# 256-byte starts for the tiles that TensorE reads, and a multiplication moved to ScalarE, in a routed expert kernel behind linear attention

## The chip, the cores and the metric

The kernel runs on one core of a Trainium2 chip. The metric is the device time of one execution in microseconds. Before the change the median of three runs is 739.91 us (738.52 to 740.43).

## The reference

Two stages, all in float32. The first is a linear attention over 8 batches, 8 heads, 576 positions and head dimension 64: queries and keys go through a feature map of 256 features (a projection of 128, the largest magnitude subtracted, exponentials of both signs), and a position's output is its features times the sum of key features by values, divided by a normalizer. The second is a mixture of experts on the 4608 tokens of width 512 that come out: a gate picks one of 8 experts for each token, by its own logits or, where a local gate says so, by taking over the choice of the token before, and the token passes through that expert's two layers:

```python
def phi(x):
    proj = np.einsum('bhsd,df->bhsf', x, w_phi)
    proj = proj - np.max(np.abs(proj), axis=-1, keepdims=True)
    return np.concatenate([np.exp(proj), np.exp(-proj)], axis=-1)
...
e = fresh_e if s == 0 or local_gate[b, s] < 0.5 else prev_e
p = softmax(logits[b, s])
h = np.maximum(x[b, s] @ w1[e], 0.0)      # 512 -> 1024
out[b, s] = p[e] * (h @ w2[e])            # 1024 -> 512
```

## The kernel before

**Two stages on the clock.** The front stage (`step`, `proj`, `qtr`, `kv`, `num`, `gate`) walks over 72 pairs of 128-position chunks, writes the tokens to HBM as `xs`, and scatters token numbers and probabilities into one list for each expert, `lst`. The expert stage takes tokens from these lists in slots: a slot is an expert and one to four tiles of 128 tokens. Two *advance slots* of three tiles each (`EARLY`) are planned in the front stage from the lists as far as they are filled; they run while the planning of the rest (`plan_main`, many small VectorE instructions, then gathers by GpSimd) goes on beside them. Then come four slots of four tiles, four of three, one of two, and between them two *paired slots*, in which two experts share one tile.

**What a slot does.** Its expert's weights come as eight pieces of 128x1024 (`load`, L1002 on, through SyncE's queue): four of the first layer, four of the second. `split` (L1023 on) makes two tiles of each piece: ScalarE rounds it to `whi` (L1032), VectorE writes the rest `wlo = wraw - whi` (L1035). Tokens, gathered by GpSimd as `xg`, are transposed by TensorE and split the same way into `xhi` and `xlo` (`parts`, L1150, L1151). For the first advance slot the same split is made in the front stage by `half` (L509, L511).

`three` (L1153 to L1157) is the expert layers' inner product: three matmuls into one PSUM accumulation, high by high, high by low and low by high.

```python
mm(o, ah, bh, start=first, stop=False)   # L1155
mm(o, ah, bl, start=False, stop=False)   # L1156, or as the operands fall
self.last_pe = mm(o, al, bh, ...)        # L1157
```

The first of the two inputs is the stationary operand (128 columns, fetched by a weight load of its own, which the profile calls PEld), the second the moving one. In `layer1` the weights are stationary and the tokens move, as 512, 384 or 256 columns with four, three or two tiles; a weight piece serves two blocks of 128 hidden units, four slices of the input and the three products, 24 matmuls. ScalarE applies the rectifier and writes `hh` (L1200), VectorE writes the rest `hl` (L1201). In `layer2` the hidden values are stationary and the weights move, always 512 columns; for each tile of tokens 24 matmuls (eight blocks, three products) fill one PSUM bank. VectorE then multiplies the bank by the tokens' probabilities into `y` (L1254), and GpSimd scatters `y` to the output by an indirect DMA (L1257). Paired slots use L1168 instead of `three`, whole float32 operands, and take their pieces straight from DMA into `whi` and `wlo`.

**Order.** TensorE's order in the front stage is the program's; from the advance slots on, a list scheduler orders each engine's instructions, led by `issue_after` and by `marks`, the last instruction of a kind on each engine, which `past` puts in front of the next split. `spare` asks for the next weight piece whenever one is used up. In the advance slots the PSUM banks of the second layer come from the pool `psb` (tag `nm`, two banks, shared with small results of the planning); later slots have a pool `psr` of their own.

**Where the tiles lie.** The allocator puts every tile at a multiple of 32 bytes of its partition. Left pools follow on the many small constants, right pools come from the far end. Start addresses, and what is left past a multiple of 256 (all tiles of a kind agree in that, and all steps inside them that a matmul takes are multiples of 256):

| tiles | pool | start addresses | past a multiple of 256 |
|---|---|---|---|
| `whi`, `wlo`, eight each | `moe_early`, left | 22176 to 83616 | 160 |
| `whi`, `wlo`, two each | `moe_wl`, left | 112288 to 124576 | 160 |
| `whi`, `wlo`, three each | `moe_wr`, right | 188384 to 208864 | 224 |
| `xhi`, `xlo` | `moe_x2`, right | 212960, 221152 | 224 |
| `hh`, `hl` | `moe_h2`, right | 149280, 165664 | 32 |
| `kvs`, three (front stage) | `back2`, left | 112288, 114528, 116768 | 160, 96, 32 |

Weight pieces take the pools' places in turn (`wpool`), so most slots have some pieces left and some right. Of the 864 matmuls of 512 columns in the second layer, 642 read left weights and 222 right ones; in the first layer 312 of 384 matmuls with 512 columns, 432 of 576 with 384 and 48 of 96 with 256 load left weights. Those that the prediction shows: the first four-tile slot's first layer (from 357.11 us) has two left pieces and then two right ones; the two-tile slot's (from 708.36) the same; the three-tile slot's first layer from 402.50 has left pieces only, the three-tile slot's second layer from 612.87 as well, and the stretch from 658.74 in a four-tile slot's second layer is three right pieces.

Of the kernel before, what the change touches and what calls it, by code (L numbers as in the profile page):

```python
# [7 lines left out]
F32 = mybir.dt.float32  # L8
F32R = mybir.dt.float32r
BF16 = mybir.dt.bfloat16  # L10
I32 = mybir.dt.int32
AF = mybir.ActivationFunctionType
# [22 lines left out]
FILL = 6  # L35
KVLAG = 1
QUOTA = 16

STEP = "step"

# [29 lines left out]
class Kernel:  # L70
# [427 lines left out]
    def halved(self, s):  # L498

        p = self.wpool()  # L500
        s["w"].append([p.tile([128, 1024], F32R, name=n) for n in ("whi", "wlo")])
        return s["w"][-1]

    def half(self, raw, whole, k):
# [8 lines left out]
    def step(self, p, n):  # L513
# [24 lines left out]
        for i in pair:  # L538
            if i % NC != 4:
                self.kv(i)  # L540
        for _ in range(min(QUOTA, len(self.todo)) if p < n // 2 else len(self.todo)):
            self.todo.pop(0)()
# [459 lines left out]
    def load(self, s, i):  # L1002


        sp = self.sp
        if "r" not in s:
            with self.past(sp):
                s["r"] = [sp.value_load(x[:, 0:1], min_val=0, max_val=E - 1) for x in s["ei"]]
            s["w"], s["raw"] = [], []
        self.rk = getattr(self, "rk", 0) + 1  # L1010
        rp = self.ml1 if hasattr(self, "ml1") and self.rk % 2 else self.mxg
        src = self.A["w1h"] if i < 4 else self.A["w2h"]
        if len(s["r"]) == 2:
            p = self.wpool()
            s["w"].append([p.tile([128, 1024], F32R, name=n).bitcast(F32) for n in ("whi", "wlo")])
            dst = s["w"][-1]
        else:
            dst = [rp.tile([128, 1024], F32, name="wraw", bufs=3 if rp is self.mxg else 2)]
            s["raw"].append(dst[0])
        for r, t in zip(s["r"], dst):  # L1020
            self.marks[sp] = sp.dma_start(t, src[bass.ds(r, 1), i % 4].rearrange("o p n -> (o p) n"))

    def split(self, s, low=None):  # L1023

        if not s["raw"]:
            return
        raw = s["raw"].pop(0)
        p = self.wpool()
        hi = p.tile([128, 1024], F32R, name="whi")
        lo = p.tile([128, 1024], F32R, name="wlo")  # L1030
        with self.past(self.act):
            self.act.copy(hi, raw)  # L1032
        for c in [slice(k, k + 256) for k in range(0, 1024, 256)] if low else [slice(0, 1024)]:
            with nullcontext() if low else self.past(self.dve):
                (low or self.dve).tensor_sub(lo[:, c], raw[:, c], hi.bitcast(F32)[:, c])  # L1035
        s["w"].append((hi, lo))
# [50 lines left out]
    def into(self, s):  # L1087
        if "x" not in s:
            p = self.mxt if s["n"] > 1 else self.ml1
            s["x"] = [p.tile([128, 4, s["n"] * 128], F32R, name=x + "1" * (s["n"] == 1)) for x in ("xhi", "xlo")]  # L1090
        return s["x"]

    def first_tokens(self, s):
# [79 lines left out]
        return self.tc.issue_after(x.ins) if x else nullcontext()  # L1173

    def hidden(self, n):
        return [self.mx2.tile([128, 8, n * 128], F32R, name=x, bufs=1) for x in ("hh", "hl")]

    def layer1(self, s, between):

# [53 lines left out]
    def layer2(self, s, between, held=None):  # L1233
        tc, dve, pool = self.tc, self.dve, self.pool
        hh, hl = s["h"]
        self.need(s, 8) if len(s["ei"]) == 1 else None
        for k in range(s["n"]):
            if hasattr(self, "psr"):
                t = self.psr.tile([128, DM], F32, name="l2")
            else:  # L1240
                t = self.psb.tile([128, DM], F32, name="l2", tag="nm")
            o = slice(k * 128, k * 128 + 128)
            for f in range(8):
                c = slice((f % 2) * DM, (f % 2) * DM + DM)
                self.both(s, 4 + f // 2, t, hh[:, f, o], hl[:, f, o], c, f == 0, f == 7)
                if f in ((0, 2) if s["n"] > 1 else (1, 3, 5)) and between:
                    between.pop(0)()
                if f % 2 and k == s["n"] - 1:
                    self.used(1)
                elif f % 2:  # L1250
                    self.spare()
            y = self.mx2.tile([128, DM], F32, name="yl", bufs=1) if held is not None else self.mx2.tile([128, DM], F32, name="y")
            u = s["u"] + k
            self.marks[dve] = dve.tensor_scalar_mul(y, t, s["prob"][:, u:u + 1])  # L1254

            def put(y=y, at=s["tok"][:, u:u + 1]):
                ins = pool.indirect_dma_start(self.A["out"], bass.IndirectOffsetOnAxis(at, 0), y, None,  # L1257
                                              bounds_check=NT - 1, oob_is_err=False)
                tc.declare_no_dep(ins.ins, group="outs", reason="each token is written once")
                tc.add_to_no_dep_group("outs", ins.ins)  # L1260
            if held is None:
                put()
            else:
                held.append(put)
# [161 lines left out]
```

## Time and profile before

| | |
|---|---|
| median of three runs | 739.91 us (738.52 to 740.43) |
| profiled execution | 738.96 us |
| its span, first to last instruction | 737.1 us |
| TensorE busy | 722.0 us, 98% of the span, 9447 matmuls |
| VectorE busy | 448.7 us, 61% |
| ScalarE busy | 344.5 us, 47% |
| GpSimd busy | 180.2 us, 24% |
| moved by DMA | 125.05 MB, 170 GB/s on average |

In the profile PE is TensorE's matmuls, PEld its weight loads, DVE VectorE, ACT ScalarE, POOL GpSimd, SP SyncE. A row of a group gives line, engine, operation, output and inputs, shapes and count, then busy time, the mean of one in ns and the idle time before, with what ended it. A row of one line or tile gives shortest, median and longest duration in ns and the first and last start. A row of the timeline gives start and duration in us, and a count behind x. Matmuls of one stream overlap in the timeline, since each is shown from its start to the modelled end of its pipeline; the distance between starts is what one of them costs.

### The profile page before, as it was taken

How to read it: one execution, taken by the hardware profiler on the slowest of the kernel's cores; microseconds unless marked ns; L12 is line 12 of the kernel's file. 1: busy time of each engine (PE TensorE's matmuls, PEld its weight loads, DVE VectorE, ACT ScalarE, POOL GpSimd, SP SyncE). 2: the span in 40 equal slices, each digit the busy share in tenths (PEclk: the TensorE clock that was granted, in tenths of full speed). 3: DMA queues.
4: the chain of work that ended last, by engine and by line, in shares of the span. 5: the costliest groups of instructions: out<-in, count | busy, mean ns of one | idle time of the engine just before them, and what ended most of it. 6: DMA issues, size and time to landing. Idle time of an engine off the chain costs nothing. (4 is left out here: it accounts for less than half of the span.)

```text
span 737.1 us, 22171 instructions
## 1 busy us (share of the span) xinstructions
PE 722.0 (98%) x9447; PEld 630.2 (86%) x9447; DVE 448.7 (61%) x820; ACT 344.5 (47%) x667; POOL 180.2 (24%) x302
## 2 busy tenths in 40 slices
PE   7999999999989999999999999999999999999996
PEld 6999999999989999888888975889888688888895
DVE  5798899889978886765454335544522456444413
ACT  4777776776668782414252315413322344241301
POOL 0200100430246676454212130120303103001011
PEclk9999999999999999999999999999999999999998
DMA  7765544555576662256739956236676464434100
GB/s 209 219 199 143 151 141 136 157 148 145 137 222 198 205 185 75 62 178 205 266 86 357 332 199 237 71 128 232 217 271 221 144 208 148 161 108 157 65 33 30
DMA packets 66101, 125.05 MB, mean 170 GB/s; under 512 B 7220, under 2 KB 45300, under 8 KB 65950
## 3 DMA queue, kind: packets, MB, share of 16 engines
q1 hardware_dynamic: 57808, 101.03, 42.9%
q0 software_dynamic: 8016, 22.51, 8.8%
q8 instruction: 75, 1.23, 0.7%
q14 instruction: 26, 0.21, 0.1%
q10 hardware_dynamic: 176, 0.07, 0.0%
HBM read 102.05 MB, written 22.06 MB: 168 GB/s over the span
## 5 line engine op out<-in xcount | busy, mean ns | idle before, releaser
L1200 ACT ACTIVATE hh<-l 128x384 fp32r<-128x384 f32 (+1 forms) x84 | 45.1, 537 | 207.3 <-PE l L1157 207.3
L1155 PE MATMUL l<-xhi,whi 128*128 128x384 f32 (+2 forms) x352 | 124.1, 353 | 0.0
L1157 PE MATMUL l<-xhi,wlo 128*128 128x384 f32 (+2 forms) x352 | 123.6, 351 | 0.0
L1156 PE MATMUL l<-xlo,whi 128*128 128x384 f32 (+2 forms) x352 | 123.3, 350 | 0.0
L1201 DVE SCALAR_TENSOR_TENSOR hl<-l,hh 128x384 fp32r<-128x384 f32 (+1 forms) x84 | 51.6, 614 | 115.5 <-ACT hh L1200 115.3
L1155 PE MATMUL l<-whi,hh 128*128 128x512 f32 x288 | 115.5, 401 | 0.6 <-DVE y L1254 0.6
L1035 DVE TENSOR_TENSOR wlo<-wraw,whi 128x1024 fp32r<-128x1024 f32 x80 | 96.5, 1223 | 29.0 <-ACT whi L1032 29.0
L1156 PE MATMUL l<-wlo,hh 128*128 128x512 f32 x288 | 113.8, 395 | 0.0
L1157 PE MATMUL l<-whi,hl 128*128 128x512 f32 x288 | 113.7, 395 | 0.0
L300 ACT ACTIVATE kp<-sb 128x512 f32<-128x512 f32 x144 | 83.3, 623 | 56.7 <-DVE sb L296 53.9
L294 DVE TENSOR_REDUCE m<-pj 128x8 f32<-128x1024 f32 x72 | 88.0, 1223 | 28.9 <-PE pj L291 27.9
L1032 ACT CAST whi<-wraw 128x1024 fp32r<-128x1024 f32 x80 | 82.1, 1046 | 37.4 <-PE l L1157 16.0
L291 PE MATMUL pj<-first,kq 64*128 64x128 f32 x1152 | 86.7, 291 | 4.7 <-DMA kq<-in_kqT 4.2
L296 DVE TENSOR_TENSOR sb<-pj,m 128x1024 f32<-128x1024 f32 x72 | 88.2, 1225 | 4.6
L419 PE MATMUL nm<-kvs,qp 128*64 128x74 f32 x2304 | 87.6, 227 | 2.1 <-issue 1.7
L324 ACT ACTIVATE qp<-pj 128x512 f32<-128x512 f32 x144 | 80.1, 596 | 13.1 <-PE pj L309 12.0
L419 PEld LDWEIGHTS nm<-kvs,qp 128*64 128x64 f32 x2304 | 80.2, 136 | 2.6 <-issue 1.9
L291 PEld LDWEIGHTS pj<-first,kq 64*128 64x128 f32 x1152 | 72.6, 193 | 11.0 <-issue 4.4
L1257 POOL DMA_INDIRECT out<-y,p_tokm x30 | 35.0, 1165 | 183.2 <-DVE y L1254 166.7
L341 PE MATMUL kvp<-v,kp 128*64 128x65 f32 x2048 | 76.9, 226 | 0.2 <-ACT kp L300 0.2
L1155 PEld LDWEIGHTS l<-xhi,whi 128*128 128x128 f32 x352 | 66.1, 188 | 7.2 <-issue 1.6
L1157 PEld LDWEIGHTS l<-xhi,wlo 128*128 128x128 f32 x352 | 66.2, 188 | 5.5
(228 smaller groups left out, 916.2 us busy)
## 6 DMA issues: line engine op xcount, KB each, us to landing
wraw<-in_w1h SPq DMA_DIRECT2D x44, 512.0 KB, 4.9
wraw<-in_w2h SPq DMA_DIRECT2D x44, 512.0 KB, 5.7
kq<-in_kqT SPq DMA_DIRECT2D x47, 384.0 KB, 4.0
v<-in_va SPq DMA_DIRECT2D x48, 195.0 KB, 3.6
xs<-xo SPq DMA_DIRECT2D x48, 128.0 KB, 2.6
whi<-in_w1h SPq DMA_DIRECT2D x8, 512.0 KB
wlo<-in_w1h SPq DMA_DIRECT2D x8, 512.0 KB, 9.1
whi<-in_w2h SPq DMA_DIRECT2D x8, 512.0 KB
```

What stands on the lines that cost most here:

```text
L291: self.last_pe = self.pe.matmul(t[:, h, i % 2, j, :], kq[r, j, s], self.w2[r], start=True, stop=True)
L294: dve.tensor_reduce(m, f, AX.X, ALU.max, apply_absolute_value=True)
L296: self.last_dve = dve.tensor_sub(sb.rearrange("p h c j f -> p (h c j) f"), f, m.unsqueeze(2).broadcast_to([128, 8, 128]))
L300: self.last_act = act.activation(kp[:, :, :, sg, :].rearrange("p c h f -> p h c f"), sb[:, :, :, 0], AF.Exp, scale=1.0 - 2 * sg)
L324: self.act.activation(qp[:, sg].rearrange("p h (c r k) -> p (h c) r k", c=2, r=2), src, AF.Exp, scale=1.0 - 2 * sg)
L341: self.pe.matmul(t[r, sg, h], kp[:, h, sg, r], v[:, h], start=first and sg + h == 0, stop=last and sg + h == 2)
L419: self.last_num = self.pe.matmul(e["t"][r, c - c0, k], self.ch[i]["qp"][:, sg, h, q0 + r.start:q0 + r.stop], kvs[:, sg, k], start=sg == 0, ...
L1032: self.act.copy(hi, raw)
L1035: (low or self.dve).tensor_sub(lo[:, c], raw[:, c], hi.bitcast(F32)[:, c])
L1155: mm(o, ah, bh, start=first, stop=False)
L1156: mm(o, ah, bl, start=False, stop=False)
L1157: self.last_pe = mm(o, al, bh, start=False, stop=last)
```

## The change

The request `align_bytes=256` is added wherever `whi`, `wlo`, `xhi`, `xlo`, `hh` and `hl` are made, so that all of these tiles start at a multiple of 256 bytes in their partition. Other tiles have no request of their own; those that follow on the weights in the left pools move by 96 bytes. In the advance slots (those that run before the pool `psr` exists) ScalarE writes `y`, as a copy scaled by the probabilities, in place of VectorE; later slots keep VectorE.

```diff
+LINE = 256
...
     def halved(self, s):
-        s["w"].append([p.tile([128, 1024], F32R, name=n) for n in ("whi", "wlo")])
+        s["w"].append([p.tile([128, 1024], F32R, name=n, align_bytes=LINE) for n in ("whi", "wlo")])
...
         if len(s["r"]) == 2:
-            s["w"].append([p.tile([128, 1024], F32R, name=n).bitcast(F32) for n in ("whi", "wlo")])
+            s["w"].append([p.tile([128, 1024], F32R, name=n, align_bytes=LINE).bitcast(F32) for n in ("whi", "wlo")])
...
-        hi = p.tile([128, 1024], F32R, name="whi")
-        lo = p.tile([128, 1024], F32R, name="wlo")
+        hi = p.tile([128, 1024], F32R, name="whi", align_bytes=LINE)
+        lo = p.tile([128, 1024], F32R, name="wlo", align_bytes=LINE)
...
-            s["x"] = [p.tile([128, 4, s["n"] * 128], F32R, name=x + "1" * (s["n"] == 1)) for x in ("xhi", "xlo")]
+            s["x"] = [p.tile([128, 4, s["n"] * 128], F32R, name=x + "1" * (s["n"] == 1), align_bytes=LINE)
+                      for x in ("xhi", "xlo")]
...
     def hidden(self, n):
-        return [self.mx2.tile([128, 8, n * 128], F32R, name=x, bufs=1) for x in ("hh", "hl")]
+        return [self.mx2.tile([128, 8, n * 128], F32R, name=x, bufs=1, align_bytes=LINE) for x in ("hh", "hl")]
...
-            self.marks[dve] = dve.tensor_scalar_mul(y, t, s["prob"][:, u:u + 1])
+            if hasattr(self, "psr"):
+                self.marks[dve] = dve.tensor_scalar_mul(y, t, s["prob"][:, u:u + 1])
+            else:
+                self.marks[self.act] = self.act.activation(y, t, AF.Copy, scale=s["prob"][:, u:u + 1])
```

## The prediction

> **What bounds the kernel now.** I read the page first: the busy times, then the slices, then the groups; after that the groups with shapes kept apart, the waits of the instructions that the change touches, and last the timeline of TensorE alone, row by row.
>
> ```profile
> span 737.1 us, 22171 instructions
> PE 722.0 (98%) x9447; PEld 630.2 (86%) x9447; DVE 448.7 (61%) x820; ACT 344.5 (47%) x667; POOL 180.2 (24%) x302
> PE   7999999999989999999999999999999999999996
> DVE  5798899889978886765454335544522456444413
> ACT  4777776776668782414252315413322344241301
> PEclk9999999999999999999999999999999999999998
> DMA  7765544555576662256739956236676464434100
> ```
>
> TensorE is busy in every slice but the first and the last, at full granted clock, while VectorE and ScalarE run half empty in the second half. The expert layers run from the first matmul of the first layer to the last of the second:
>
> ```profile
> L1155 PE MATMUL l<-xhi,whi x352: 278/336/502, 283.9 to 719.4; 128*128 128x384 f32 x96, 128*128 128x512 f32 x64, 128*128 128x256 f32 x16
> L1155 PE MATMUL l<-whi,hh x288: 390/394/505, 301.8 to 730.4; 128*128 128x512 f32 x144
> ```
>
> That is 284 to 731 us. In that stage the engine has hardly a gap to lose, so its time is the number of matmuls times their spacing. The groups give the numbers.
>
> ```profile
> L1155 PE MATMUL l<-whi,hh 128*128 128x512 f32 x288 | 115.5, 401 | 0.6 <-DVE y L1254 0.6
> L1156 PE MATMUL l<-wlo,hh 128*128 128x512 f32 x288 | 113.8, 395 | 0.0
> L1157 PE MATMUL l<-whi,hl 128*128 128x512 f32 x288 | 113.7, 395 | 0.0
> L1155 PE MATMUL l<-xhi,whi 128*128 128x384 f32 x192 | 64.7, 339 | 0.0
> L1155 PE MATMUL l<-xhi,whi 128*128 128x512 f32 x128 | 50.4, 393 | 0.0
> L1155 PE MATMUL l<-xhi,whi 128*128 128x256 f32 x32 | 9.0, 281 | 0.0
> L1156 PEld LDWEIGHTS l<-wlo,hh 128*128 128x128 f32 x288 | 54.2, 188 | 12.0 <-DVE wlo L1035 0.4
> ```
>
> The second layer (moving `whi` or `wlo`, stationary `hh` or `hl`) is 3 x 288 = 864 matmuls of 512 columns; the first layer (moving `xhi` or `xlo`, stationary `whi` or `wlo`) is 3 x 128 = 384 of 512 columns, 3 x 192 = 576 of 384 and 3 x 32 = 96 of 256. Idle time before them is 0.6 us in all, behind one `y`. What the durations hide, since matmuls overlap, is the spacing of starts. So I looked for stretches in which nothing but these matmuls runs, and read the first and the last start of each.
>
> **The change part by part. First: the offsets.** The section on the kernel lists where the tiles begin: past a multiple of 256 bytes, x at 224, hidden at 32, left weights at 160, right weights at 224. The change puts all of them at 0, so each pair of operands that a matmul and the weight load beside it read is then at equal offsets. No trace has that layout; but one stretch already has equal offsets: the first layer with right weights (224 and 224). It follows directly on one with left weights (224 and 160), with the same moving tiles and the same 512 columns:
>
> ```profile
> 357.11 0.40 PE L1155 MATMUL l<-xhi,whi 128*128 128x512 f32 x1
> ...
> 367.88 0.40 PE L1157 MATMUL l<-xhi,wlo 128*128 128x512 f32 x1
> 368.11 0.39 PE L1155 MATMUL l<-xhi,whi 128*128 128x512 f32 x1
> ...
> 378.78 0.39 PE L1157 MATMUL l<-xhi,wlo 128*128 128x512 f32 x1
> ```
>
> Each stretch is 48 starts (two weight pieces of 2 blocks x 4 slices x 3). Left weights: (367.88 - 357.11) / 47 = 229.1 ns. Right weights: (378.78 - 368.11) / 47 = 227.0 ns. The second layer, whose hidden tile is at 32, first from left weights (68 starts in a three-tile slot), then from right ones (18 starts in a four-tile slot):
>
> ```profile
> 612.87 0.39 PE L1156 MATMUL l<-wlo,hh 128*128 128x512 f32 x1
> ...
> 628.43 0.39 PE L1157 MATMUL l<-whi,hl 128*128 128x512 f32 x1
> ...
> 658.74 0.40 PE L1155 MATMUL l<-whi,hh 128*128 128x512 f32 x1
> ...
> 662.72 0.39 PE L1157 MATMUL l<-whi,hl 128*128 128x512 f32 x1
> ```
>
> Left: 15.56 / 67 = 232.2 ns. Right: 3.98 / 17 = 234.1 ns. Put in order of the difference of offsets (moving minus stationary, modulo 256), the four kinds stand so: 0 gives 227.0, 64 gives 229.1, 128 gives 232.2, 192 gives 234.1. I read it as one effect: the streaming read and the weight load for the next matmul disturb each other the less, the nearer their starts lie within 256 bytes. At difference 0 everywhere, the 512-column matmuls should all stand at 227.0.
>
> From the layout, 642 of the 864 second-layer matmuls read left weights and 222 right ones; 312 of the 384 first-layer ones are loaded from left. That is 642 x 5.2 = 3.34 us, 222 x 7.1 = 1.58 us and 312 x 2.1 = 0.66 us: 5.6 us less. Narrower matmuls need rows of their own, since a gain is not certain there:
>
> ```profile
> 402.50 0.33 PE L1155 MATMUL l<-xhi,whi 128*128 128x384 f32 x1
> ...
> 418.96 0.34 PE L1157 MATMUL l<-xhi,wlo 128*128 128x384 f32 x1
> ...
> 708.36 0.28 PE L1155 MATMUL l<-xhi,whi 128*128 128x256 f32 x1
> ...
> 713.90 0.28 PE L1157 MATMUL l<-xhi,wlo 128*128 128x256 f32 x1
> 714.01 0.28 PE L1155 MATMUL l<-xhi,whi 128*128 128x256 f32 x1
> ...
> 719.64 0.28 PE L1157 MATMUL l<-xhi,wlo 128*128 128x256 f32 x1
> ```
>
> At 384 columns, 96 starts from left weights: 16.46 / 95 = 173.3 ns. Against the equal-offset 227.0 at 512 columns that is 53.7 ns for 128 columns, 0.42 ns each, so both sit on one line with the same 12 ns on top: nothing is left to remove there, and I take zero. At 256 columns (48 starts each) left weights give 5.54 / 47 = 117.9 ns and right ones 5.63 / 47 = 119.8: here equal offsets are slower by 1.9 ns, which costs 48 x 1.9 = 0.1 us. The sum for the offsets is 5.6 - 0.1 = 5.5 us. Its bounds: zero if the second layer is slow for another reason, 6 if the disturbed stretches that I left out gain too.
>
> The Trainium skill's page "TensorE: Matmul & The Clock Gate" (section "Step-by-step: what each phase is for") speaks against this: the stream and the weight load have independent SBUF read ports, so that loading the next weights takes nothing from the running matmul. By it the offsets are worth nothing; the trace disagrees, since 229.1 and 227.0 ns stand side by side with only the stationary operand's place changed.
>
> The request moves other tiles: everything on the left behind the constants goes up by 96 bytes, `kvs` in the front stage among them. L419 shows what that may do:
>
> ```profile
> L419 PE MATMUL nm<-kvs,qp x2304: 224/227/279, 23.9 to 283.7; 128*64 128x74 f32 x192
> ```
>
> Its `kvs` has three buffers at 160, 96 and 32, yet the shortest of 2304 and the median are 3 ns apart. I take zero for the front stage; half a nanosecond each would be 1.2 us, either way. The paired slots' transfers into `whi` and `wlo` begin aligned too; they have no term, since TensorE hardly waits for weights (0.4 us in the row for `wlo` above).
>
> **Second: the multiplication.** It concerns six instructions in the advance slots: VectorE loses them, ScalarE gains them.
>
> ```profile
> L1254 DVE TENSOR_SCALAR y<-l,p_probe x6: 736/748/753, 315.4 to 357.4; 128x512 f32<-128x512 f32 x6
> ```
>
> ```profile
> L1200 ACT ACTIVATE hh<-l 128x512 fp32r<-128x512 f32 x36 | 21.5, 598 | 98.9 <-PE l L1157 98.9
> ```
>
> ```profile
> 315.43 0.74 DVE L1254 TENSOR_SCALAR y<-l,p_probe 128x512 f32<-128x512 f32 x1
> 315.88 1.05 ACT L1032 CAST whi<-wraw 128x1024 fp32r<-128x1024 f32 x1 [3.33 <-DMA wraw<-in_w2h]
> 316.22 0.51 PE L1155 MATMUL l<-whi,hh 128*128 128x512 f32 x1 [0.63 <-DVE y L1254]
> ```
>
> VectorE saves 6 x 0.748 = 4.5 us, ScalarE spends about 6 x 0.60 = 3.6 us (an estimate by its nearest row, 128x512 out of PSUM). Neither engine is the bound, so both sums are worth nothing by themselves. What counts is the last row: the third tile's accumulation needs the PSUM bank that the first `y` empties, and that `y` stood behind the planning arithmetic on VectorE until 315.43. ScalarE had idled 3.33 us for a transfer just then. The stall of 0.63 us goes; what is late next is nothing that I see. Behind a `y` that waits on ScalarE stand the next slot's `whi` casts, and VectorE's `wlo` behind these; the casts wait for their transfers anyway, as the row of 315.88 shows. Bounds: 0.8 won, if matmuls bunched around the stall move too, and 0.6 lost, one `y` ahead of a cast that is needed at once. I take 0.6.
>
> **The sum.** 5.5 + 0.6 = 6.1 us. The profiled execution took 738.96 us (its span 737.1 and 1.9 around it), and would take 732.9; it lies 0.95 below the median of the three runs, 739.91, which then becomes 733.8.
>
> **The rivals.** *It is the layer and not the offset.* The second layer reads weights as moving operand and runs beside VectorE's and ScalarE's splitting of the next slot, which could cost it the 5 to 7 ns. For it speaks that each layer has its own pair of values. Against it, left and right weights differ within each layer while the work beside is the same. Then 0.66 + 0.6 - 0.1 = 1.2 us remain: 738.7, and 739.3 if the first layer does not follow either. The SBUF page of the Trainium skill (section "Specifications (TRN2)") has 16-byte lines, of which all the old starts were multiples already; by it too only the 0.6 remains, and the rows above disagree with that as far as the first layer goes.
>
> *Half of it.* Distance in SBUF matters beside the offset within 256 bytes: right weights lie near x, left weights far from everything, and the equal-offset stretch is also the near one. If only half of the 4.9 us of the second layer comes, 739.91 - 2.5 - 0.7 - 0.6 + 0.1 = 736.2.
>
> *Slower.* Reads that start in step collide instead of interleaving. The place is every weight load beside a stream, and 256 columns show it already: equal offsets 119.8 against 117.9. If that +1.9 ns held for all 864 + 312 + 432 matmuls whose offsets become equal (432 of the 576 with 384 columns are loaded from left), it would cost 3.1 us, 742.4 with the 0.6 off. It decides as soon as the 512-column spacing rises above about 233 ns; the 227.0 at equal offsets speaks against it.
>
> *Much better.* A start at 0 could also take off the 12 ns that remain over 0.42 per column; 1824 matmuls x 12 are 22 us, 712. No row hints at it: 224 and 224 keep the 12.
>
> **How the numbers follow.** The forecast 733.8 has 0.68. The half has 0.12, the layer 0.13, slower 0.04, much better 0.03. A measurement of this kernel tells a change from none at about 0.3%, 2.2 us. Faster by more: 0.68 + 0.12 + 0.03 = 0.83; within: 0.13; slower by more: 0.04. The range begins at 739.91 - 6.4 - 0.8 and another 0.9 for runs, 731.8; it ends with the half and 1.1 for runs and the front stage, 737.3. Outside lie the layer, slower and much better, 0.20.
>
> **What would show it.** In the changed kernel's timeline, stretches of second-layer matmuls spaced 227 ns whatever pool their weights are in, and no longer 232 to 234; the means of the three second-layer groups (401, 395, 395) down by about 5, to those of the first layer; 384 columns still at 173.3; L1254 on ACT six times near 600 ns and no 0.63 us behind it; the expert layers shorter by 6 us and the front stage as before. Wrong would be a second layer still above 230, or a wait for `whi` or `wlo` that eats what the spacing gives.

## The result, and the profile after

Over nine runs of each kernel the median goes from 738.95 us to 732.9 us. The ratio of the times is 0.9928, with a 95% interval from 0.9913 to 0.9942: 5.3 us less (4.3 to 6.4), where the prediction had 6.1. The two medians by themselves lie 6.0 us apart; the ratio is what the interval belongs to.

The page of the changed kernel, in the rows that answer to those of before:

```profile
span 729.5 us, 22170 instructions
PE 714.6 (98%) x9447; PEld 627.9 (86%) x9447; DVE 444.8 (61%) x814; ACT 348.4 (48%) x673; POOL 180.9 (25%) x302
PE   7999999999999999999999999999999999999996
PEclk9999999999999999999999999999999999999998
```

TensorE is still the bound, at the same clock, with the same 9447 matmuls; only its busy time fell. VectorE's and ScalarE's counts moved by six, from 820 to 814 and from 667 to 673. The groups by shape (busy us, mean ns, idle before):

```profile
L1157 PE MATMUL l<-whi,hh 128*128 128x512 f32 x288 | 114.1, 396 | 0.0
L1158 PE MATMUL l<-wlo,hh 128*128 128x512 f32 x288 | 112.4, 390 | 0.0
L1159 PE MATMUL l<-whi,hl 128*128 128x512 f32 x288 | 112.3, 390 | 0.0
L1157 PE MATMUL l<-xhi,whi 128*128 128x384 f32 x192 | 64.8, 338 | 0.0
L1157 PE MATMUL l<-xhi,whi 128*128 128x512 f32 x128 | 49.9, 390 | 0.0
L1157 PE MATMUL l<-xhi,whi 128*128 128x256 f32 x32 | 9.1, 283 | 0.0
```

The second layer's means are down by 5 each, from 401, 395 and 395, and stand where the first layer's with 512 columns stand. The idle 0.6 us before the first row, put down to `y`, is gone. The spacing of starts is what counts; the timeline of TensorE has it, for the first layer of the first four-tile slot (96 starts) and the second layer of a three-tile slot (68 starts):

```profile
353.64 0.39 PE L1157 MATMUL l<-xhi,whi 128*128 128x512 f32 x1
...
375.17 0.39 PE L1159 MATMUL l<-xhi,wlo 128*128 128x512 f32 x1
...
512.11 0.39 PE L1158 MATMUL l<-wlo,hh 128*128 128x512 f32 x1
...
527.30 0.39 PE L1159 MATMUL l<-whi,hl 128*128 128x512 f32 x1
```

(375.17 - 353.64) / 95 = 226.6 ns, and (527.30 - 512.11) / 67 = 226.7 ns: both layers alike. Over the whole kernel the second layer stands at 227.5 ns with left weights and 227.1 with right ones. It is longer in the advance slots, which run beside the planning: 229.4 ns there and 227.1 in all later slots, where the kernel before had 232.5 and 232.7. So equal offsets bring less in the advance slots; the runs don't show why. First and last start of the expert layers, from the views of the lines L1157 and L1159:

```profile
L1157 PE MATMUL l<-xhi,whi x352: 278/334/496, 281.6 to 711.6; 128*128 128x384 f32 x96, 128*128 128x512 f32 x64, 128*128 128x256 f32 x16
L1159 PE MATMUL l<-whi,hl x288: 388/389/398, 300.0 to 722.9; 128*128 128x512 f32 x144
```

They take 722.9 - 281.6 = 441.3 us, against 446.9 before (first start 283.88, last start 730.81): 5.6 us less. The two spans differ by 7.6 us: the expert layers also begin 2.3 us earlier, and what follows them is 0.3 us longer. TensorE's 200th matmul starts 1.3 us earlier here than in the profile of before, and in the profile of the kernel with the old offsets (`e2_y_only` below) it does as well; such starts differ from one execution to the next. Where the other 1.0 us comes from is not shown; the 4.3 to 6.4 us of the nine runs leave no room for all of the 7.6. The front stage's `kvs` moved by 448 bytes (to 112736, 114976 and 117216), and not by 96 as the section on the change and the prediction have it. Its matmuls did not change their pace: their line, L420 now, has 224, 227 and 279 ns as shortest, median and longest, as L419 had before.

### The profile page after: what moved, and what is told of

Same layout as the page of the kernel before. It is cut to its first block, busy times and chain, and to the rows that moved or that the text cites. A ratio compares the mean times of both kernels' runs of the same rounds, so it can differ in the third digit from the quotient of the medians.

```text
span 729.5 us, 22170 instructions
## 1 busy us (share of the span) xinstructions
PE 714.6 (98%) x9447; PEld 627.9 (86%) x9447; DVE 444.8 (61%) x814; ACT 348.4 (48%) x673; POOL 180.9 (25%) x302
## 5 line engine op out<-in xcount | busy, mean ns | idle before, releaser
L1157 PE MATMUL l<-xhi,whi 128*128 128x384 f32 (+2 forms) x352 | 123.8, 352 | 0.0
L1159 PE MATMUL l<-xhi,wlo 128*128 128x384 f32 (+2 forms) x352 | 123.2, 350 | 0.0
L1157 PE MATMUL l<-whi,hh 128*128 128x512 f32 x288 | 114.1, 396 | 0.0
L1159 PE MATMUL l<-whi,hl 128*128 128x512 f32 x288 | 112.3, 390 | 0.0
L420 PE MATMUL nm<-kvs,qp 128*64 128x74 f32 x2304 | 87.5, 227 | 2.0 <-issue 1.6
L420 PEld LDWEIGHTS nm<-kvs,qp 128*64 128x64 f32 x2304 | 80.1, 136 | 2.5 <-issue 1.8
L1157 PEld LDWEIGHTS l<-xhi,whi 128*128 128x128 f32 x352 | 66.2, 188 | 7.1 <-issue 1.6
L1158 PEld LDWEIGHTS l<-xlo,whi 128*128 128x128 f32 x352 | 66.2, 188 | 5.1
```

The lines of the kernel that those rows point to most:

```text
L420: self.last_num = self.pe.matmul(e["t"][r, c - c0, k], self.ch[i]["qp"][:, sg, h, q0 + r.start:q0 + r.stop], kvs[:, sg, k], start=sg == 0, ...
L1159: self.last_pe = mm(o, al, bh, start=False, stop=last)
```

## The experiments

**How the spacing is measured.** Where a spacing stands for a whole kernel, it is the mean distance between successive starts of these matmuls in the profile, leaving out distances over 260 ns (a transpose or a wait in between). "Expert layers" is the time from their first start to their last. Times are compared with runs of the kernel before on the same chip; its median was 737.95 us for the first four kernels and 743.12 for `e5` to `e7`, and one run took 743.34 for `e8` and `e9`. `e4` and `e6` to `e9` were run once each.

**The parts alone.** `e1_offsets_only` is the changed kernel with VectorE's multiplication back:

```diff
-            if hasattr(self, "psr"):
-                self.marks[dve] = dve.tensor_scalar_mul(y, t, s["prob"][:, u:u + 1])
-            else:
-                self.marks[self.act] = self.act.activation(y, t, AF.Copy, scale=s["prob"][:, u:u + 1])
+            self.marks[dve] = dve.tensor_scalar_mul(y, t, s["prob"][:, u:u + 1])
```

> The 256-byte starts alone; VectorE keeps the advance slots' multiplication. Theory A (the spacing follows the difference of the two operands' offsets): second layer near 227 ns, gain 5.0 to 5.6 us against the kernel before, and the 0.6 us stall behind the first y is back, so 0.5 to 0.8 us slower than the changed kernel. Rival B (the order that follows from y on ScalarE brought a good part): gain under 4 us although the spacing is 227.

Measured: 733.59 us, ratio 0.9946 (0.9931 to 0.9961), 4.0 us less. Second layer 227.5 ns, first layer 226.8 ns, expert layers 442.3 us: 4.6 less than before and 1.0 more than with both parts, where 0.5 to 0.8 was expected. The wait is back, as the group by shape shows:

```profile
L1157 PE MATMUL l<-whi,hh 128*128 128x512 f32 x288 | 114.3, 397 | 0.7 <-DVE y L1256 0.7
```

The gain is below the 5.0 to 5.6 us that theory A set, and sits on B's limit; its size is taken up by the next kernel, which gives B nothing. `e2_y_only` has the old layout (a request for 32, the allocator's own step, moves nothing) and ScalarE's multiplication:

```diff
-LINE = 256
+LINE = 32
```

> y on ScalarE alone, all tiles where they lay before. Theory A: spacing 232 to 234 ns in the second layer as before, no stall of 0.6 us behind the first y, gain 0.5 to 0.8 us. Rival B: gain of 1.5 us or more.

Measured: 737.62 us, ratio 0.9993 (0.9979 to 1.0006), no difference that the runs can tell. Second layer 232.4 ns with left weights and 233.5 with right ones; expert layers 446.1 us, 0.9 less than before, no wait behind `y`. So the expert layers give 4.6 for the offsets and 0.9 for `y`, 5.5 of the 5.6 together: the parts add up and B, which asked for 1.5 us from `y`, falls by the profiles. The times alone (from 1.5 us less to 0.4 more) would hardly decide it.

**Equal, or on a boundary?** All the tiles at 0 are both. `e3_equal_at_160` separates them: 64 bytes of padding in each of two pools bring every kind to 160.

```diff
-LINE = 256
+LINE = 32
+PADX, PADH = 16, 16
...
+            s["x"] = [p.tile([128, n + PADX * (x == "xlo" and n > 512)], F32R, name=x + "1" * (n == 512))[:, 0:n].rearrange(
+                "p (d c) -> p d c", d=4) for x in ("xhi", "xlo")]
...
+        return [self.mx2.tile([128, n * 1024 + PADH * (x == "hl")], F32R, name=x, bufs=1)[:, 0:n * 1024].rearrange(
+            "p (f c) -> p f c", f=8) for x in ("hh", "hl")]
```

> y on ScalarE; no request for 256, but 64 bytes of padding in two pools, so that weights, x and hidden tiles all lie 160 bytes past a multiple of 256 (32 past one of 64). Theory A, which asks for equal offsets only: spacing 227 ns in the second layer and with 512 columns in the first, time within 1 us of the changed kernel. Rival C, which asks for starts on a boundary (of 64 or 256 bytes): spacing 232 ns, gain against the kernel before under 1.5 us.

Measured: 732.69 us, ratio 0.9928 (0.9911 to 0.9945), the changed kernel's own. Second layer 227.4 ns, first 226.7; expert layers 441.3 us. The groups by shape are the changed kernel's to the nanosecond:

```profile
L1159 PE MATMUL l<-whi,hh 128*128 128x512 f32 x288 | 114.1, 396 | 0.0
L1160 PE MATMUL l<-wlo,hh 128*128 128x512 f32 x288 | 112.4, 390 | 0.0
L1161 PE MATMUL l<-whi,hl 128*128 128x512 f32 x288 | 112.3, 390 | 0.0
```

A start 160 bytes past a multiple of 256, which is not even a multiple of 64, is as good as one at 0. The boundary does nothing; equality within 256 bytes brings the gain. Rival C falls.

The opposite: `e5_hidden_at_128` leaves every other tile at 0 and moves the hidden tiles, by half of 256. (Its x tiles are 256 bytes longer and still start at 0, and so are those of `e7` below.)

```diff
+        o, n = 32 * (n > 1), n * 1024
+        return [self.mx2.tile([128, n + 64], F32R, name=x, bufs=1, align_bytes=LINE)[:, o:o + n].rearrange(
+            "p (f c) -> p f c", f=8) for x in ("hh", "hl")]
```

> The changed kernel with the hidden tiles moved by 128 bytes, so that in the second layer alone the operands differ by 128 (0 and 128, both on boundaries of 128). Theory A (equal offsets): second layer at 232.3 ns, first layer at 226.8, so 864 x 4.9 = 4.2 us slower than the changed kernel, gain against the kernel before 1 to 2 us. Rival C (starts on a boundary): nothing changes, gain still 5 us or more.

Measured: second layer 232.5 ns, first layer 226.8, as A has it. The groups by shape have the second layer back at the means of before, and the first layer at those of the changed kernel:

```profile
L1158 PE MATMUL l<-whi,hh 128*128 128x512 f32 x288 | 115.4, 401 | 0.0
L1159 PE MATMUL l<-wlo,hh 128*128 128x512 f32 x288 | 113.8, 395 | 0.2 <-DVE wlo L1036 0.2
L1160 PE MATMUL l<-whi,hl 128*128 128x512 f32 x288 | 113.7, 395 | 0.0
...
L1158 PE MATMUL l<-xhi,whi 128*128 128x512 f32 x128 | 49.9, 390 | 0.0
```

The expert layers take 446.0 us, 4.7 more than in the changed kernel. The time, 739.36 us against 743.12, is 3.4 us less than before (0.9954, 0.9939 to 0.997): more than A's 1 to 2, less than C's 5. Against the 446.9 us of before, the expert layers account for only 0.9 us of that. No profile of the kernel before was taken on that chip, so the other 2.5 us stay open. The offsets of `e5` are not needed for such a gap: `e8` below, with the old offsets and expert layers of 446.7 us, took 3.3 us less than a run of before beside it. The mean granted clock may have part in it, which is not shown: it was 0.996 or 0.997 in the eleven runs of before, 0.998 or 0.999 in five of the six of `e5`, and the sixth, at 0.995, took 742.25 us.

**Which difference costs how much?** `e4_sweep` keeps the weights at 0 and starts hidden and x tiles elsewhere in each slot, inside tiles 256 bytes longer; `e6_sweep_at_160` does the same over the layout with everything at 160.

```diff
+HIDS = [32, 64, 96, 128, 160, 192, 224, 16, 48, 240, 8]
+XS = [32, 96, 64, 160, 128, 224, 192, 16, 32, 48, 128]
...
+            n, o = s["n"] * 512, self.xos.pop(0) // 4 if s["n"] > 1 else 0
...
+        o, n = self.hids.pop(0) // 4 if n > 1 else 0, n * 1024
```

> Weights at 0; the hidden tiles begin at another offset in each slot (32, 64, 96, 128, 160, 192, 224, 16, 48, 240, 8) and the x tiles too (512 columns: 64, 128, 192, 32). Theory A: the spacing rises with moving minus stationary modulo 256 as in the kernel before: hidden at 192 (difference 64) about 229, at 128 about 232, at 64 (difference 192) about 234, small differences near 227; x at 64, 128, 192 the same three values. Rival C: a step between multiples of 64 and the rest (32, 96, 160, 224, 16, 48, 8 near 232, the multiples of 64 at 227).

> The sweep again with weights at 160 instead of 0; hidden at another offset in each slot, x too (512 columns: 224, 192, 32, 96). It asks why a difference of 64 gave 229 in the kernel before and 233 in the first sweep. Theory A1 (the two absolute starts count beside their difference): x at 224 gives 229 again, and hidden at 96, also a difference of 64 with both starts 32 past a multiple of 64, gives 229 as well. Rival A2 (any difference costs 5 to 7 ns, and the 229 belonged to those tiles' distance in SBUF): x at 224 gives 229, hidden at 96 gives 233. Both: difference 128 near 232, nothing but equal offsets at 227.

Measured, for 512 columns, in ns; the difference is moving minus stationary, modulo 256. Values are of the longest stretch in a slot without a break, read as above from its first and last start:

| difference | weights at 0 | weights at 160 | kernel before |
|---|---|---|---|
| 0 | 226.7 (changed kernel) | 226.7 (`e3`) | 227.0 |
| 8 | | 233.3 | |
| 16 | 228.3 | 228.5 | |
| 32 | 233.3, 233.2 | 233.3, 233.4 | |
| 64 | 233.3, 233.3 | 233.3, 229.2 | 229.1 |
| 96 | 233.3 | 233.4 | |
| 128 | 232.3, 232.4 | 232.3, 232.4 | 232.2 |
| 160 | 234.3 | 234.2 | |
| 192 | 233.4, 233.7 | 233.3, 233.4 | 234.1 |
| 208, 224, 240 | 233.3, 233.5, 233.3 | 233.3 (224), 233.3 (240) | |
| 248 | 230.4 | 230.6 | |

Where two values stand in a cell of one sweep, the first is of the first layer and the second of the second. The whole kernels took 738.83 us (`e4`, 737.95 before) and 742.86 us (`e6`, 743.12 before), one run each. With the first sweep's x at 64, a first layer of 96 starts, the timeline reads:

```profile
354.72 0.40 PE L1161 MATMUL l<-xhi,whi 128*128 128x512 f32 x1
...
376.89 0.40 PE L1163 MATMUL l<-xhi,wlo 128*128 128x512 f32 x1
```

That is 22.17 / 95 = 233.4 ns, at a difference for which the kernel before had 229.1. So the spacing does not rise with the difference. It is a pit at 0, with 232 to 234 nearly everywhere else, and it depends on the difference and hardly on the places: the columns for 0 and 160 agree within 0.3 ns but for one value at 64. Both theories of the first sweep fail: A's slope, and C's 227 at every multiple of 64. The pit is narrow: with the moving operand 8 bytes above the stationary one, or 16 below it, the whole 6.6 is paid; 16 above costs 1.6 to 1.8, and 8 below 3.7 to 3.9. The kernel before owes its 229 to a value that the difference 64 takes in some stretches only. Theory A1 had 229 for x at 224 and for hidden at 96 in the second sweep and got 233.3 and 229.2; A2 had 229 and 233, and fails twice. `e8_x_256_apart` tried one more reason, the old layout with `xhi` and `xlo` no longer at the same place within 512 bytes:

```diff
+            s["x"] = [p.tile([128, n + 64 * (x == "xhi" and n > 512)], F32R, name=x + "1" * (n == 512))[:, 0:n].rearrange(
+                "p (d c) -> p d c", d=4) for x in ("xhi", "xlo")]
```

> The old layout with y on ScalarE, but xhi 256 bytes longer, so that xhi and xlo no longer lie at the same place within 512 bytes; within 256 all offsets are the old ones (x 224, left weights 160). It asks why a difference of 64 gave 229 in the kernel before and 233 in both sweeps, whose x tiles were 256 bytes longer too. Theory M (for unequal offsets the place within 512 bytes counts as well): first layer with left weights and 512 columns near 233. Rival N (the sweeps' other changes did it): 229 again. Both: 227 with right weights, second layer 232 to 234 as before.

Measured: 229.1 ns with left weights, 227.0 with right ones, second layer 232.7; one run, 740.06 us against 743.34. Theory M falls. What makes a difference of 64 cost 2 ns in one layout and 6 in another is open.

**Whose weights?** Two kernels move one tile of a pair by 128 bytes, `hl` or `xlo`, so that one matmul in three is odd.

```diff
+        return [self.mx2.tile([128, n + 64], F32R, name=x, bufs=1, align_bytes=LINE)[:, o * (x == "hl"):o * (x == "hl") + n].rearrange(
```

> The changed kernel with hl alone moved by 128 bytes; hh stays at 0. The second layer runs hh-whi, hh-wlo, hl-whi. Theory A (the stream of one matmul is disturbed by the weight load for the next one): only the distance from the second matmul (during which hl is loaded) to the third is long, 232 or more, the other two stay at 227. Rival D (a matmul is slow because of its own stationary operand): only the distance after the third, whose stationary operand is hl, is long. Mean 228.5 to 230 in both.

```diff
+            s["x"] = [p.tile([128, n + 32 * o], F32R, name=x + "1" * (n == 512), align_bytes=LINE)[:, 32 * o:n + 32 * o].rearrange(
+                "p (d c) -> p d c", d=4) for x, o in (("xhi", 0), ("xlo", n > 512))]
```

> The changed kernel with xlo alone moved by 128 bytes. The first layer runs whi-xhi, whi-xlo, wlo-xhi, so only the second of three matmuls streams from another offset than the weights before and after it. Theory P (a stream is slowed where the stationary operand it runs on, or the one loaded beside it, lies at another offset): with 512 columns only the distance after the second is long, 232 or more, the others at 227. Rival Q (a change of offset from one stream to the next is what costs): the distances after the first and the second are long.

The timeline of TensorE in `e7_hl_at_128`, second layer (hh-whi, hh-wlo, hl-whi, and again):

```profile
655.44 0.39 PE L1158 MATMUL l<-whi,hh 128*128 128x512 f32 x1
655.67 0.40 PE L1159 MATMUL l<-wlo,hh 128*128 128x512 f32 x1
655.90 0.40 PE L1160 MATMUL l<-whi,hl 128*128 128x512 f32 x1
656.13 0.39 PE L1158 MATMUL l<-whi,hh 128*128 128x512 f32 x1
```

The timeline rounds to 10 ns; the means over the kernel are 227.3 ns after the first matmul, 232.3 after the second and 234.0 after the third. Theory A expected only the second to be long, rival D only the third; both are, and the mean of 231.2 is above either's 230. In `e9_xlo_at_128`, first layer with 512 columns, the means are 228.9, 234.2 and 226.8 ns (737.67 and 735.44 us for the two kernels, single runs):

```profile
360.13 0.39 PE L1158 MATMUL l<-xhi,whi 128*128 128x512 f32 x1
360.36 0.40 PE L1159 MATMUL l<-xlo,whi 128*128 128x512 f32 x1
360.60 0.39 PE L1160 MATMUL l<-xhi,wlo 128*128 128x512 f32 x1
```

There the second is long, as P has it. In three of the four four-tile slots the first stands at 226.7 and the third at 225.6 to 226.0. In the other slot all three are long, 236, 234 and 230. The first and last start of that slot's first layer, and then of another's:

```profile
451.52 0.40 PE L1159 MATMUL l<-xlo,whi 128*128 128x512 f32 x1
...
473.46 0.39 PE L1160 MATMUL l<-xhi,wlo 128*128 128x512 f32 x1
...
626.01 0.39 PE L1158 MATMUL l<-xhi,whi 128*128 128x512 f32 x1
...
647.76 0.39 PE L1160 MATMUL l<-xhi,wlo 128*128 128x512 f32 x1
```

(473.46 - 451.52) / 94 = 233.4 ns against (647.76 - 626.01) / 95 = 228.9. Both slots have the same offsets, and the weight pieces from 456.89 and from 626.01 even lie in the same two buffers. So at unequal offsets the start addresses alone do not fix the spacing. The 229 and 233 at a difference of 64 may be such a pair; that is not shown.

P fits `e7` and three of the four slots of `e9`: a stream is slowed if the stationary operand that it runs on, or the one loaded beside it, lies at another offset. In `e7` the second stream has `hl` loaded beside it and the third runs on `hl`; in `e9` only the second stream is at odds with its weights. Rival Q would have the first long in every slot. What makes the fourth slot differ, and why the operand in use still counts, once it is loaded, these runs don't show.

## Why the prediction was right, point by point

**The bound.** Right: the gap-free TensorE stage carried its gain to the end, and no wait for weights took the place of what went.

**The offsets.** The step that read the old rows as a cause in the operands' offsets was right, and `e3` and `e5` show it: equal offsets give 227 ns wherever they lie, and undoing them in one layer gives that layer its 232 back. The prediction's reason, that the stream and the load for the next matmul disturb each other, covers only part of it: in `e7` the third stream had 234.0 ns though the weights loaded beside it lay at its own offset. The size was 5.5 us, and 4.6 came (expert layers of `e1`). The second layer was mis-sized: at 227.4 to 227.5 ns as a mean over the kernel it stays 0.4 above the 227.0 of the one stretch that I took, because of the 229.4 of the advance slots, and right weights had stood at 233.5 over all, not at the 234.1 of theirs. By these means it brought 642 x 4.9 + 222 x 6.1 = 4.5 us for the 4.9 predicted. The first layer with 512 columns brought 312 x 2.3 = 0.7 as predicted. Two small losses stand against that: 576 matmuls with 384 columns went from 173.7 to 173.8 ns, 0.1 us where zero was taken, and 48 with 256 columns from 117.9 to 119.9, the 0.1 foreseen. That makes 5.0; the 0.4 down to 4.6 lies in the distances over 260 ns, which sum to 58.5 us in `e1` and to 57.9 us before. The zero for 384 columns came out nearly right on a weak reason: two points, 384 and 512, lie on one line whatever they are, and only the 119.8 at 256 columns was a test of it. The bounds give 6 us as the most that the offsets bring, while the range takes 6.4; with 6 it would begin at 732.2.

**The order of the differences.** "The streaming read and the weight load disturb each other the less, the nearer their starts lie" is the sentence that was wrong. Four values in rising order were chance: the sweeps show a pit at 0, not a slope. The forecast did not need the slope, since it goes only to 0; had the change aimed at "nearly equal", the slope would have promised a gain where 8 bytes already give 233.3.

**The multiplication.** 0.6 us was taken for the stall and 0.8 was the bound; 0.9 came with the old offsets (446.9 to 446.1, rounded) and 1.0 with the new (442.3 to 441.3). In the changed kernel the first `y` runs where ScalarE waited for TensorE:

```profile
L1259 ACT ACTIVATE y<-l,p_probe x6: 683/690/690, 306.4 to 353.9; 128x512 f32<-128x512 f32 x6
306.37 0.69 ACT L1259 ACTIVATE y<-l,p_probe 128x512 f32<-128x512 f32 x1 [1.84 <-PE l L1159]
```

It starts at 306.4, 9 us before it did on VectorE (7 us, counted from the first start of the expert layers), so the bank was free long before TensorE came back for it. One of them takes 690 ns, not the 600 of the estimate; that it costs nothing was right. No cast behind it was late: TensorE's idle time before its second layer is 0.0.

**The rivals.** "The layer and not the offset" fell, since both layers now stand within 1 ns of each other. The half fell as well: left and right weights now stand within 0.5 ns of each other, so at equal offsets distance in SBUF hardly counts. "Slower" was right about 256 columns, made 0.1 ns of its 1.9 at 384 and was wrong at 512. "Much better" had no trace: the 12 ns over 0.42 per column remain, at 0 as at 160.

The Trainium skill's page "TensorE: Matmul & The Clock Gate" (section "Step-by-step: what each phase is for") holds that loading the next weights takes nothing from the running matmul. The runs disagree: in the second layer `e5` differs from the changed kernel in the hidden tiles' start alone, and it pays 5 ns more for each of the 864 matmuls. Whether the load takes nothing at equal offsets no run shows, since every matmul here has one.

**The sum.** 6.1 us predicted, 5.6 us in the expert layers, 5.3 (4.3 to 6.4) by the runs: an offset term too large by 0.9 and a `y` too small by 0.3 to 0.4.

## What to carry to other kernels

Where TensorE runs without gaps and each matmul has its own weight load, compare the spacing of starts between groups of the same shape, and look at the operands' start addresses modulo 256: here, moving and stationary operands at different offsets cost 1 to 3% of the 512-column time (228 to 234 ns against 227), and with 256 columns they cost nothing. What is asked for is equality within 256 bytes, not a boundary, so one common remainder for all tiles does as well as a request for 256. An accumulation bank whose reader stands in a long queue is worth moving to the idle engine, but only for about the length of the wait that the profile puts down to it (0.6 us here, and 0.9 to 1.0 gained).

## What the runs showed of the hardware that had not been expected

A difference of 8 bytes between the two operands' starts costs as much as one of 96: 233.3 against 226.7 ns for 512 columns (`e6`), while 16 bytes cost 1.6 to 1.8 with the moving operand at the higher place and 6.6 with it at the lower (`e4` and `e6` alike). With 256 columns unequal offsets are the faster ones, 117.8 to 118.6 ns against 119.9. The place within 256 bytes itself does not count at equal offsets: 226.7 at 0 and at 160. At unequal ones, one kernel has 228.9 and 233.4 ns for the same addresses in two slots (`e9`).
